# Attention with a leaky-ReLU feed-forward on one core: the feed-forward of all batches and the scores and AV of batches 3 to 8 as pairs of 64-row matmuls, and PSUM as four double banks

## The chip, the cores and the metric

The kernel runs on one core of a Trainium2 chip. A core has a matrix engine (PE), which reads weights (PEld) and streams a second operand past them into PSUM, and four others: VectorE (DVE), ScalarE (ACT), GpSimd (POOL, here mostly an issuer of DMAs and of memsets) and SyncE (SP, here an issuer of DMAs). Each has its own queue of instructions and works it off in order. PSUM has eight banks of 128 partitions x 512 fp32.

The metric is the device time of one execution in microseconds; a lower number is better. The time quoted for a kernel is the median of its runs.

## The reference

Eight batches of eight heads of attention with a relative-position bias, then a feed-forward on 4608 tokens:

```python
scores = scale * np.matmul(q, k.transpose(0, 1, 3, 2))          # q, k, v: (8, 8, 576, 64)
bias = bias_table[bucket]                                       # bucket of |i - j|; one value from distance 128 on
scores = scores + bias.transpose(2, 0, 1)[None]
attn = softmax(scores)                                          # exp(s - max) / (sum + 1e-9)
x = np.matmul(attn, v).transpose(0, 2, 1, 3).reshape(4608, 512)
h = x @ w_in                                                    # w_in: (512, 2048)
out = np.maximum(0.01 * h, h) @ w_out                           # w_out: (2048, 512)
```

All inputs and the output are fp32 in HBM; the kernel works in bf16 with fp32 sums.

## The kernel before

The attention runs over 32 items n: batch n // 4 and a pair of heads, n % 4. The two heads of a pair lie in the lower and the upper 64 partitions of `qt` and `kt` (head dimension on the partitions, 576 positions on the free axis). For an item:

- `rows`, `turn_by_pe` or `turn_by_dma`, `take_turned`: q and k are turned so that the head dimension lies on the partitions, by the PE up to item 8 (but 7) and by DMA transposes on SP's queue from then on.
- `score(n, u)`, six units: u = 0 to 3 are 128 keys each against queries 0 to 511, two matmuls of 64 rows x 512 columns, one for each head, into two banks of one `ps_s` buffer (L424). u = 4 is queries 512 to 575 of both heads, four matmuls of 128 rows x 128 columns, where `own` has zeroed the other head's half (L428). u = 5 is the last 64 keys of both heads, one matmul of 128 rows x 512 columns and one of 64 columns (L431, L432).
- `expo` (ACT): exp out of PSUM into `at` and `at4`; `band` (DVE): times exp(bias) in the band of 128 around the diagonal.
- `av`: for both heads e five chunks of queries, each four matmuls of 128 rows (keys) x 65 columns (64 of v, one of ones for the sum; L493). The last 64 keys come from `av_tail` as ten matmuls of 64 rows (L478) in items 4 to 30, and in the other items as 128-row matmuls that have zeros in the other head's half of `v4` (L496). One head's sums go to `ps_o`, the other's to `ps_o` or `ps_om`.
- `norm` (DVE): a reciprocal and a product for each head, into `opair`. Then `x_pe` and `x_copy` (items 0 to 5, 7 and 31) or `x_dma` (a DMA transpose on SP's queue) put it into `xT`, 512 features in four chunks of 128 partitions, all 4608 tokens.

The feed-forward runs over nine tiles T of 512 tokens. `ffn_in(T, f)`: four matmuls of 128 rows x 512 columns for each of 16 chunks f (L536), `ffn_act` on ACT into `gt`. `ffn_out(T, ts, i)`: for each of four groups of 128 tokens, 16 matmuls of 128 rows x 512 columns (L561), four to a step i; `ffn_y` on DVE copies the sum to SBUF, `ffn_store` writes it to HBM by SP's queue. The last group of tokens is cut into columns (`ffn_end`, L547).

PSUM has two `ps_s` buffers of two banks each, one bank `ps_o` and three single banks (`ps_m_pool`, tag "m") that hold `ps_om`, the turned tiles and all sums of the feed-forward.

The order on PE, ACT, DVE, POOL and SP is written out ahead of the run by `Plan`: each piece of work is a task (`add`) with an engine, a cost, the tasks it comes after, a rank, and the PSUM slots that it takes and gives ("S", "O", "M"). `Plan.order` places tasks by their time of readiness and rank; `SHIFT`, `HOLD` and `SWAP` correct single tasks by their number. The hardware then runs the written order with semaphores. While attention goes on, steps of the feed-forward stand on the PE between units of attention; what is left of it follows the last item. Up to 26 us, matmuls on `junk` (`spin`, L814) fill waits of the PE.

## Time and profile before

| | |
|---|---|
| median of 3 runs | 375.99 us (375.4 to 376.88) |
| the profiled execution's own time | 375.4 us |
| its span | 373.5 us |
| ACT busy | 243.7 us (65%) |
| DVE busy | 204.0 us (55%) |
| output stores (SP's queue), each 256 KB | 35, median 2.0 us to landing |
| turns of q and k by DMA | 24, median 6.2 us to landing |
| `xT` by DMA | 24, median 3.1 us to landing, 10.9 us at most |

A row of groups in the profile has the line, the engine, the operation, what it writes and reads with the shape, how often (x), its busy time, the mean duration of one in ns, and the idle time of its engine ahead of it. A matmul's duration is longer than the distance to the next one, since matmuls overlap in the array; rows of the timeline show starts, from which distances can be taken. In a row of the timeline that stands for several matmuls (x8), the time is from the start of the first to the end of the last.

### The profile page before, as it was taken

The page shows a single profiled execution, that of the slowest core. Times are in us where ns is not written, and L with a number is a line of the kernel's source. Part 1 is how long each engine was busy: PE and PEld are TensorE (multiplying, and loading weights), DVE is VectorE, ACT ScalarE, POOL GpSimd, SP SyncE. Part 2 cuts the span into 40 slices and gives each one's busy share as a digit, 9 for nine tenths or more (in the row PEclk, how much of TensorE's full clock was granted, in tenths as well). Part 3 has the DMA queues.
Part 4 walks back from the last instruction along what each step waited for, and adds up shares of the span by engine and source line. Part 5 has one row for each costly group of instructions (what it writes and reads, how often), then busy time and mean ns, then how long its engine had stood idle before and what let it go on. Part 6 is the DMA issues. An engine that isn't in the chain of part 4 may idle for free.

```text
span 373.5 us, 8628 instructions
## 1 busy us (share of the span) xinstructions
PE 368.0 (99%) x3556; PEld 191.7 (51%) x3556; DVE 204.0 (55%) x550; ACT 243.7 (65%) x351; POOL 69.4 (19%) x107
## 2 busy tenths in 40 slices
PE   8999999999999999999999999999999999999996
PEld 5675555545555555545555555545555544444444
DVE  7997567786786557655755676555643311001021
ACT  5998987588756995697667866977678333333300
POOL 8856023340025003500350013000000000000000
PEclk9999999999999999999999999999999999999999
DMA  8999999999469907991899159201210101001012
GB/s 121 156 181 197 185 181 114 212 212 176 64 132 183 177 18 111 189 157 20 131 198 146 30 113 137 71 11 47 75 47 20 47 28 54 32 28 58 28 56 86
DMA packets 103735, 39.51 MB, mean 106 GB/s; under 512 B 83472, under 2 KB 98192, under 8 KB 103696
## 3 DMA queue, kind: packets, MB, share of 16 engines
q0 software_dynamic: 53424, 18.21, 46.2%
q1 hardware_dynamic: 49920, 20.39, 29.1%
q8 instruction: 28, 0.46, 0.5%
q10 hardware_dynamic: 352, 0.36, 0.3%
q14 instruction: 11, 0.09, 0.1%
HBM read 36.70 MB, written 9.44 MB: 124 GB/s over the span
## 4 chain that ended last, share of the span: by engine, by line
PE 95%; ACT 3%; DVE 1%; issue 1%; POOL 0%; POOLq 0%
PE pm L536 34%; PE pm L561 33%; PE ps_s L424 9%; PE ps_om L493 6%; PE ps_o L493 5%; ACT at L438 2%; PE ps_s L428 2%; PE ps_s L431 2%; PE pm L547 1%; PE ps_o L478 1%; PE ps_tx L520 1%; PE ps_t L382 0%; DVE hots L301 0%; PE ps_t L387 0%; PE ps_w L814 0%
## 5 line engine op out<-in xcount | busy, mean ns | idle before, releaser
L438 ACT ACTIVATE at<-ps_s 128x1024 bf16<-128x1024 f32 x124 | 120.4, 1028 | 32.8 <-PE ps_s L424 32.8
L536 PE MATMUL pm<-xT,w_in_sb 128*128 128x512 bf16 x576 | 140.8, 379 | 0.0
L561 PE MATMUL pm<-w_out_sb,gt 128*128 128x512 bf16 x560 | 135.5, 379 | 0.0
L540 ACT ACTIVATE gt<-pm 128x512 bf16<-128x512 f32 x144 | 84.8, 605 | 59.8 <-PE pm L536 58.8
L458 DVE TENSOR_TENSOR at<-at,hk 128x768 bf16<-128x768 bf16 (+4 forms) x156 | 69.5, 453 | 64.0 <-ACT at L438 47.1
L561 PEld LDWEIGHTS <-gt 128*128 128x128 bf16 x560 | 52.5, 98 | 64.7 <-issue 5.1
L536 PEld LDWEIGHTS <-w_in_sb 128*128 128x128 bf16 x576 | 52.2, 98 | 63.1 <-issue 6.4
L566 DVE COPY y<-pm 128x512 f32<-128x512 f32 x35 | 24.2, 691 | 70.6 <-PE pm L561 70.6
L236 POOL DMA_DIRECT2D vn<-in_v_dram x32 | 28.9, 911 | 141.3 <-PE ps_o L493 131.0
L493 PEld LDWEIGHTS <-at 128*128 128x128 bf16 x1240 | 41.2, 98 | 3.7 <-issue 0.7
L424 PE MATMUL ps_s<-qt,kt 64*128 64x512 bf16 x256 | 40.0, 381 | 0.3
L440 ACT ACTIVATE at<-ps_s 128x512 bf16<-128x512 f32 x31 | 18.7, 602 | 16.7 <-PE ps_s L428 16.6
L493 PE MATMUL ps_o<-vn,at 128*128 128x65 bf16 x640 | 25.5, 193 | 0.0
L493 PE MATMUL ps_om<-vn,at 128*128 128x65 bf16 x600 | 24.1, 195 | 0.0
L424 PEld LDWEIGHTS <-kt 64*128 64x128 bf16 x256 | 8.3, 94 | 24.7 <-issue 22.0
L445 ACT ACTIVATE at<-ps_s 128x576 bf16<-128x576 f32 x31 | 20.3, 654 | 0.8 <-PE ps_s L432 0.7
L506 DVE TENSOR_TENSOR opair<-ps_o,rcp 128x320 bf16<-128x320 f32 (+2 forms) x34 | 16.4, 482 | 1.2
L506 DVE TENSOR_TENSOR opair<-ps_om,rcp 128x320 bf16<-128x320 f32 (+2 forms) x32 | 15.4, 481 | 1.1
L399 DVE COPY kt<-tu 128x576 bf16<-128x576 bf16 x24 | 15.9, 663 | 0.0
L399 DVE COPY qt<-tu 128x576 bf16<-128x576 bf16 x23 | 15.0, 652 | 0.0
L505 DVE RECIPROCAL rcp<-ps_om 128x5 f32<-128x5 f32 (+2 forms) x32 | 6.1, 192 | 15.3 <-PE ps_om L493 15.3
L228 POOL DMA_DIRECT2D kn<-in_k_dram x17 | 12.1, 715 | 9.0 <-DMA w_in_sb<-in_moe_w_in_dram 3.9
(86 smaller groups left out, 238.3 us busy)
## 6 DMA issues: line engine op xcount, KB each, us to landing
out_dram<-y SPq DMA_DIRECT2D x35, 256.0 KB, 2.0
vn<-in_v_dram POOLq DMA_DIRECT2D x32, 128.0 KB, 6.9
qn<-in_q_dram POOLq DMA_DIRECT2D x14, 288.0 KB, 10.4
kn<-in_k_dram POOLq DMA_DIRECT2D x14, 288.0 KB, 10.8
w_in_sb<-in_moe_w_in_dram POOLq DMA_DIRECT2D x2, 1024.0 KB, 11.5
w_out_sb<-in_moe_w_out_dram POOLq DMA_DIRECT2D x2, 1024.0 KB, 19.6
qn<-in_q_dram POOLq DMA_DIRECT2D x4, 144.0 KB, 4.0
v<-in_v_dram POOLq DMA_DIRECT2D x16, 32.0 KB, 7.4
```

What stands on the lines that cost most here:

```text
L236: nc.gpsimd.dma_start(out=vn[i][:, c, :, 0:D], in_=v[b, :, c * P : (c + 1) * P, :].rearrange("h s d -> s h d"),)
L399: copy(out=t[:, 0:S].rearrange("p (r c) -> p r c", c=NC), in_=src)
L424: nc.tensor.matmul(ps[:, e, :], lhsT=kt[r, u * P : (u + 1) * P], rhs=qt[r, 0:512], start=True, stop=True)
L438: nc.scalar.activation(at[:, :, u, 0:512], ps, AF.Exp, scale=scale)
L445: nc.scalar.activation(at4[:, 0:S], ps.rearrange("p e i -> p (e i)")[:, 0:S], AF.Exp, scale=scale)
L458: nc.vector.tensor_tensor(out=o, in0=o, in1=m, op=ALU.mult)
L493: nc.tensor.matmul(ps[:, ic, :], lhsT=at[:, o : o + P], rhs=vn[i][:, c, 2 * p + e, :], start=whole and c == 0, stop=not whole and ic == NJ ...
L506: nc.vector.tensor_tensor(out=opairs[n][:, lo:hi, e * D : (e + 1) * D], in0=ps[:, lo:hi, 0:D], in1=rcp.to_broadcast([P, hi - lo, D]), op=A ...
L536: nc.tensor.matmul(pms[T, f], lhsT=w_in_sb[:, c, f * P : (f + 1) * P], rhs=xT[c][:, t0 : t0 + w], start=(c == 0), stop=(c == n_cc - 1))
L540: nc.scalar.activation(gts[T][:, f, :], pms.pop((T, f)), AF.Prelu, bias=0.0, scale=1.0, alpha=0.01)
L561: nc.tensor.matmul(ys[T, ts], lhsT=gts[T][:, f, ts * P : (ts + 1) * P], rhs=w_out_sb[:, f, :], start=(f == 0), stop=(f == n_fc - 1))
L566: nc.vector.tensor_copy(out=y, in_=ys[T, ts])
```

## The change

1. **Feed-forward.** x is held as eight chunks `xT[:, j, :]`: the lower 64 partitions have head j, the upper 64 the other head of its pair, so each head stands in both halves. It is a ring of four batches and no longer holds all eight. `w_in_sb` has the weights of the first eight f in its lower half and those of the last eight in its upper half, with the heads in the same order. `ffn_in(T, f)` makes 8 pairs of 64-row matmuls: the lower gives chunk f, the upper chunk f + 8, in two banks; `ffn_act` takes both at once (1024 columns, eight times a tile). `ffn_out` makes two partial sums, one for each half of the rows, in two banks; `ffn_half` (ACT) copies one to SBUF and `ffn_y` (DVE) adds the other.
2. **Scores.** u = 4 is eight 64-row matmuls of 64 columns in all items. u = 5 from item 8 on is two turns of two 64-row matmuls of 288 columns; in the second turn each half writes the bank that the other wrote in the first. `own` is no longer applied to q.
3. **AV.** From item 8 to 30, `av_half`: two turns of 40 64-row matmuls; in turn 0 each half of the rows serves one head, in turn 1 the other. `av_tail` starts every item with ten 64-row matmuls. Both heads go to one double bank. Items 0 to 7 and 31 keep 128-row matmuls (`av_full`).
4. **Guard between turns.** Both halves write the same bank in turn, so that turn 1 must not begin before turn 0 has ended. `look` (DVE) reads one element of a later score unit out of PSUM (unit 2 of the next item for AV, unit 3 for u = 5), and turn 1 waits for it.
5. **x.** `norm` takes both heads at once. By DMA (now items 4 to 31) `swap_heads` (DVE) makes a copy with the heads swapped, and two transposes are issued. By PE (items 0 to 3) there is a second turn of ten transposes of 64 columns each and a second copy. From batch 4 on the transposes come after the `ffn_in` that reads the part of the ring that they overwrite.
6. **PSUM.** Four tiles of two banks each; slots are given out by number, "S" and "O" of two banks, "M" and "N" of one in the first part. AV takes an "S" slot from item 16 on.
7. `load_w_in` issues three DMAs for each half and not one; `y` has three buffers and not four; `SHIFT`, `HOLD` and `SWAP` are new for the new numbers of tasks.

```diff
+    RING = 4
+    xT = per.tile([P, H, RING * S + P - SL], BF16, name="xT")
+    w_in_sb = per.tile([P, H, DF // 2], BF16, name="w_in_sb")
+    pairs_ = [ps_pool.tile([P, 2, 512], FP32, name=f"ps{i}") for i in range(4)]
...
+        if u == NJ:
             for c in range(NJ):
-                nc.tensor.matmul(ps[:, 0, c * P : (c + 1) * P], lhsT=kt[:, c * P : (c + 1) * P],
-                                 rhs=qt[:, S : S + P], start=True, stop=True)
+                for e in range(2):
+                    r = slice(e * D, (e + 1) * D)
+                    nc.tensor.matmul(ps[:, e, c * SL : (c + 1) * SL], lhsT=kt[r, c * P : (c + 1) * P],
+                                     rhs=qt[r, 512:S], start=True, stop=True)
...
+    def score_tail(n, turn):
...
+        for e in range(2):
+            r, x = slice(e * D, (e + 1) * D), (e + turn) % 2
+            nc.tensor.matmul(ps[:, x, 0:HS], lhsT=kt[r, S : S + P], rhs=qt[r, x * HS : (x + 1) * HS],
+                             start=(turn == 0), stop=(turn == 1))
+
+    def look(n, u):
+        nc.vector.tensor_copy(out=mark, in_=scores[n, u][0:1, 0, 0:1])
...
+    def av_half(n, turn, ics):
...
+        ps = outs[n] if turn else av_tail(n, ics)
+        for ic in (ics if turn == 0 else reversed(ics)):
             for c in range(NJ):
+                for g in range(2):
+                    e = (g + turn) % 2
+                    r = slice(g * SL, (g + 1) * SL)
+                    o = (e * NJ + c) * S + ic * P
+                    nc.tensor.matmul(ps[:, e, ic * W1 : (ic + 1) * W1], lhsT=at[r, o : o + P],
+                                     rhs=vn[i][r, c, 2 * p + e, :], start=False,
+                                     stop=turn == 1 and ic == ics[0] and c == NJ - 1)
...
+    def swap_heads(n):
+        o = opairs[n]
+        t = swapped[n] = op_pool.tile([P, NJ + 1, 2 * D], BF16, name="swapped")
...
-            out=xT[p][:, b * S : b * S + w].rearrange("p (i t) -> p i t", t=P),
-            in_=opairs[n].rearrange("p i d -> p (i d)"),
+            out=xT[:, 2 * p + e, b % RING * S : b % RING * S + w].rearrange("p (i t) -> p i t", t=P),
+            in_=(opairs, swapped)[e][n].rearrange("p i d -> p (i d)"),
...
+        for j in js:
+            for g in range(2):
+                r = slice(g * D, (g + 1) * D)
+                nc.tensor.matmul(pms[T, f][:, g, :], lhsT=w_in_sb[r, j, f * P : (f + 1) * P], rhs=x_cols(T, r, j),
+                                 start=(j == 0), stop=(j == H - 1))
...
+        nc.scalar.activation(gts[T][:, f::HF, :], pms.pop((T, f)), AF.Prelu, bias=0.0, scale=1.0, alpha=0.01)
...
         for f in range(4 * i, 4 * i + 4):
-            nc.tensor.matmul(ys[T, ts], lhsT=gts[T][:, f, ts * P : (ts + 1) * P], rhs=w_out_sb[:, f, :],
-                             start=(f == 0), stop=(f == n_fc - 1))
+            for g in range(2):
+                r = slice(g * D, (g + 1) * D)
+                nc.tensor.matmul(ys[T, ts][:, g, :], lhsT=gts[T][r, f, ts * P : (ts + 1) * P], rhs=w_out_sb[r, f, :],
+                                 start=(f == 0), stop=(f == n_fc - 1))
+
+    def ffn_half(T, ts):
+        outs["y"] = y_pool.tile([P, DM], FP32, name="y")
+        nc.scalar.copy(out=outs["y"], in_=ys[T, ts][:, 1, :])
 
     def ffn_y(T, ts):
-        y = y_pool.tile([P, DM], FP32, name="y")
-        nc.vector.tensor_copy(out=y, in_=ys[T, ts])
+        y = outs.pop("y")
+        nc.vector.tensor_tensor(out=y, in0=ys[T, ts][:, 0, :], in1=y, op=ALU.add)
...
+            if u == 2 and split:
+                mk = add("DVE", 0.1, [t], lambda: look(n, 2), rank - 30)
+                split[1]["after"].append(mk)
+                split[1]["proof"] = mk
+            if u == 3 and not tail5:
+                mk = add("DVE", 0.1, [t], lambda: look(n, 3), rank - 30)
+                t5 = add("PE", 0.13, [t, mk], lambda: score_tail(n, 1), first, proof=mk)
...
+            sw = add("DVE", 0.3, [nm], lambda: swap_heads(n), soon + 4)
+            xt[n] = [add("SP", 0.1, [d], lambda e=e: x_dma(n, e), soon + 4, tail=6.0) for e, d in ((0, nm), (1, sw))]
...
+            half = add("ACT", 0.53, last_p + ([yts[-3]] if len(yts) > 2 else []), lambda ts=ts: ffn_half(T, ts), 0)
+            y = add("DVE", 0.65, last_p + [half], lambda ts=ts: ffn_y(T, ts), 0, give=["O"], of=[(o, 0)])
```

More of the change, by code (lines that the diff above doesn't have):

```diff
@@ L74, in link @@
             t["after"] = [d for d in t["after"] if not any(d is o for o in t["behind"])]
+            if t["give"] and not t["of"]:
+                t["of"] = [(next(d for d in t["after"] if d["take"]), j) for j in range(len(t["give"]))]
     def order(self):
@@ L122, in order @@
             held = {k: sorted(slots[k]) for k in set(t["take"])}
-            r = max([r] + [s[t["take"].count(k) - 1] for k, s in held.items()])
+            r = max([r] + [s[t["take"].count(k) - 1][0] for k, s in held.items()])
             ring = self.place(t, r, free, slots, ring)
@@ L136, in place @@
         t["idle"] = r - free.get(e, 0.0)
+        t["room"] = min([x for k in "SMNO" for x in slots[k]], key=lambda x: x[0], default=(1e9, 0))
+        if t["room"][0] > free.get(e, 0.0) + 0.1:
+            t["room"] = None
         free[e] = r + cost
+        t["got"] = []
         for k in t["take"]:
[L139 to L141 removed]
+            x = min(slots[k])
+            slots[k].remove(x)
+            t["got"].append(x[1])
+        for k, (o, j) in zip(t["give"], t["of"]):
+            slots[k].append((t["end"] + self.LAG, o["got"][j]))
         return ring
@@ L148, in run @@
                 k = round(t["idle"] / 0.22) if t["start"] < 8.5 else int((t["idle"] - 0.1) / 0.11)
-                if k > 0:
-                    fill(k)
+                if k > 0 and t["room"]:
+                    fill(k, t["room"][1])
+            self.now, made = t, len(self.code())
             t["go"]()
+            if t["engine"] in ("ACT", "DVE"):
+                t["code"] = self.code()[-1]
+            elif t["proof"]:
+                self.follow(self.code()[made], t["proof"]["code"])
 @with_exitstack
@@ L704, in plan_pair @@
+            if u < 5 or tail5:
+                es[u] = add("ACT", ac[u], [t], lambda u=u: expo(n, u), rank + 2, give=spent if u == 4 else ["S"], of=[(t, 0)])
+        if not tail5:
+            ss.append(t5)
         sct[n] = ss
@@ new lines, in plan_turns @@
+        def plan_turns(after, at, ics):
+            lo, hi = ics[0] * P, min(ics[-1] * P + P, S)
+            w, xs, cs = len(ics) / 5, [], []
+            for turn in range(2):
+                x = add("PE", (0.36, 0.4)[turn] * w, after, lambda turn=turn: x_pe(n, turn, ics), at + 1, take=["M"], wide=True)
+                t = add("DVE", 0.07 + 0.35 * w, [x], None, at, give=["M"], of=[(x, 0)])
+                t["go"] = lambda t=t, turn=turn: x_copy(n, turn, t, lo, hi)
+                t["other"] = ("ACT", 0.22 + 0.31 * w)
+                xs.append(x)
+                cs.append(t)
+            return xs, cs
```

372 lines of the change are left out of this document (200 added, 172 removed), and 18 rows, old and new, of tables (HOLD, SHIFT).

## The prediction

> **What bounds the kernel now.** I read the page's shares and its chain of waits first, then the windows, then the timeline of the PE over one item.
>
> ```profile
> PE 368.0 (99%) x3556; PEld 191.7 (51%) x3556; DVE 204.0 (55%) x550; ACT 243.7 (65%) x351; POOL 69.4 (19%) x107
> ...
> PE 95%; ACT 3%; DVE 1%; issue 1%; POOL 0%; POOLq 0%
> ```
>
> The PE holds 95% of the chain that ended last. Its busy share proves little, since a matmul's duration covers the start of the next, so I look at distances between starts in one item of the steady stage.
>
> ```profile
> 117.84 0.77 PE L493 MATMUL ps_o<-vn,at 128*128 128x65 bf16 x20
> 118.45 1.89 PE L536 MATMUL pm<-xT,w_in_sb 128*128 128x512 bf16 x8
> 120.18 0.39 PE L428 MATMUL ps_s<-qt,kt 128*128 128x128 bf16 x4
> 120.40 0.38 PE L431 MATMUL ps_s<-qt,kt 128*128 128x512 bf16 x1
> 120.61 0.19 PE L432 MATMUL ps_s<-qt,kt 128*128 128x64 bf16 x1
> 120.64 1.89 PE L536 MATMUL pm<-xT,w_in_sb 128*128 128x512 bf16 x8
> 122.47 0.60 PE L424 MATMUL ps_s<-qt,kt 64*128 64x512 bf16 x4
> 123.00 2.76 PE L536 MATMUL pm<-xT,w_in_sb 128*128 128x512 bf16 x12
> 125.70 0.60 PE L424 MATMUL ps_s<-qt,kt 64*128 64x512 bf16 x4
> 126.14 0.19 PE L478 MATMUL ps_o<-v,at 64*128 64x65 bf16 x1
> 126.15 0.19 PE L478 MATMUL ps_om<-v,at 64*128 64x65 bf16 x1
> ...
> 126.26 0.19 PE L478 MATMUL ps_o<-v,at 64*128 64x65 bf16 x1
> 126.27 0.19 PE L478 MATMUL ps_om<-v,at 64*128 64x65 bf16 x1
> 126.39 0.79 PE L493 MATMUL ps_om<-vn,at 128*128 128x65 bf16 x20
> 127.01 0.77 PE L493 MATMUL ps_o<-vn,at 128*128 128x65 bf16 x20
> 127.62 1.24 PE L536 MATMUL pm<-xT,w_in_sb 128*128 128x512 bf16 x5
> ```
>
> An item repeats after 9.17 us (118.45 to 127.62). Its prices:
> - 128 x 512: the eight from 118.45 are over at 120.18, so 0.216 us each. 28 of them: 6.05.
> - Units 4 and 5 of the scores: 120.18 to 120.64, 0.46; unit 4 alone (four of 128 columns) 0.22.
> - A change between 128 and 64 rows: 120.64 + 8 x 0.216 = 122.37, but the 64-row scores start at 122.47; two pairs of them at 0.216 would end at 122.90, but the feed-forward starts at 123.00. So 0.10 each way, and again at 125.59 to 125.70 and 126.29 to 126.39: four in an item, 0.40.
> - A pair of 64-row matmuls costs what one 128-row matmul does: its halves start 0.01 or less apart (126.14, 126.15). Pairs of 65 columns: 126.14 to 126.26 is four, 0.030 each. Pairs of 512: 125.70 to 126.14 is two, 0.22 each by rows that round to 0.01.
> - AV: 40 of 128 rows, 126.39 to 127.62, 1.23, or 0.031 each; tail five pairs, 0.15.
>
> Sum: 6.05 + 0.46 + 0.40 + 4 x 0.216 + 1.23 + 0.15 = 9.15 of 9.17. The item is PE work and nothing else.
>
> ```profile
> core 0: us, PE busy (x) PEld busy (x) DVE busy (x) ACT busy (x) POOL busy (x), PEclk, DMA share, GB/s
> 118.45:127.62 9.17, 9.17 (x99) 4.65 (x96) 5.18 (x16) 8.21 (x14) 0.00 (x0) 1.00 1.36 205
> 31.93:370.50 338.57, 338.57 (x3035) 170.99 (x3031) 176.80 (x460) 217.16 (x313) 46.06 (x60) 1.00 0.70 101
> 31.93:118.45 86.52, 86.52 (x895) 44.91 (x892) 62.50 (x168) 64.91 (x91) 25.67 (x34) 1.00 1.30 164
> ```
>
> The same prices laid on the whole written order from the first feed-forward matmul (31.93) to the last matmul give 338 us, and the stage took 338.57. The granted clock (PEclk) is 1.00 throughout. So under 1 us of the stage is waiting, and anything taken off the PE's order there comes off the time, as long as no wait replaces it.
>
> **The change part by part.** The sum goes against the profiled execution's 375.4 us.
>
> *Items 8 to 30, 23 of them.* Everything is in 64 rows, so all four changes of rows go: -0.40. Unit 4 becomes four pairs of 64 columns, by the 65-column pairs 0.030 each: 0.22 to 0.12, -0.10. Unit 5 was 0.24 and becomes two pairs of 288 columns; by columns 288/512 x 0.216 = 0.12 each, 0.24: nothing. Tail and AV: 1.38 becomes 45 pairs at 0.030, 1.35: -0.03. Together -0.53, or **-12.2 us**. Unknown is a run of 98 small matmuls where the trace shows ten: its bounds are 0.015 for one matmul (half of the 0.030 above) and the distance of narrow 128-row matmuls,
>
> ```profile
> 7.56 1.01 PE L318 MATMUL ps_u<-diag,hots 128*128 128x32 bf16 x32
> L318 PE MATMUL ps_u<-diag,hots 128*128 128x32 bf16 x96 | 3.3, 177 | 0.2 <-DVE hots L301 0.2
> ```
>
> (1.01 - 0.18) / 31 = 0.027. I take 0.015, the nearest row in shape and rows.
>
> *Feed-forward.*
>
> ```profile
> L536 PE MATMUL pm<-xT,w_in_sb 128*128 128x512 bf16 x576 | 140.8, 379 | 0.0
> L561 PE MATMUL pm<-w_out_sb,gt 128*128 128x512 bf16 x560 | 135.5, 379 | 0.0
> ```
>
> These 1136 matmuls become 1136 pairs. A pair of 512 columns lies between 0.216 and the 0.22 to 0.23 that the roundings allow (two pairs and a change in 0.53, 122.47 to 123.00). I take 0.216, since the 128-row price also is pure column count (128 columns 0.055, 512 columns 0.216): 0 us, with an upper bound of 1136 x 0.01 = +11. Speaking against it, the Trainium skill ("TensorE: Matmul & The Clock Gate", section "The mechanism") says that weight loads overlap running matmuls only where the row group differs; consecutive pairs use the same two groups. By that rule each pair would show its load, at most the 0.030 of a small pair, and the sum would be 34 higher; but in the tail two loads and two matmuls on the same groups fit into 0.030 with nothing added, so the trace does not agree with it.
>
> *Items 4 to 7 and 31.* Unit 4: 5 x -0.10. They keep two to four changes of rows, about as before, save that 31 loses about two (-0.2). The PE transposes of x for 4, 5, 7 and 31 go to DMA: 20 transposes at 0.055, -1.1. Together **-1.8**.
>
> *Items 0 to 3.* Ten more narrow transposes each, about 0.28 by five of 128 columns: +1.1; some 14 more changes of rows: +1.4; unit 4: -0.4; so +2.1 on the PE. Here the PE is not full:
>
> ```profile
> 29.67 0.20 PE L496 MATMUL ps_o<-v,at 128*128 128x65 bf16 x1 [0.72 <-issue]
> 30.06 0.18 DVE L505 RECIPROCAL rcp<-ps_o 128x4 f32<-128x4 f32 x1 [1.00 <-PE ps_o L496]
> L524 DVE COPY xT<-ps_tx 128x576 bf16<-128x576 bf16 x6 | 2.7, 450 | 1.5 <-PE ps_tx L520 1.5
> L814 PE MATMUL ps_w<-junk 128*128 128x256 bf16 x36 | 6.8, 324 | 1.2 <-DVE junk L261 1.2
> ```
>
> There is the 0.72 wait and filler work on junk, that can shrink. But the second turn and the second copy (0.45) stand in the chain ahead of the first feed-forward. From 0 to +2.5; I take **+1.2**.
>
> *Guards.* Turn 1 of AV and of unit 5 wait on PE for a DVE read, 47 times. Path: a 512-column matmul lasts 0.38, so its end is 0.16 past the next start; 0.04 to the DVE (29.83 + 0.19 to 30.06 for a waiting reciprocal); the smallest read of PSUM 0.18 (that row); back about 0.06: 0.44. In the built order 41 of the 47 have eight or more feed-forward matmuls in between (four pairs, 0.86) and cost nothing while the DVE is free; without that cover each would cost 0.44. Six have at most one narrow pair (0.12): 0.32, and for a DVE busy 5.18 of 9.17 with operations near 0.5 another 0.14: 6 x 0.46 = 2.8. For covered ones that meet a late DVE, 0.7. **+3.5**, bounds 1.9 (six at 0.32) and 47 x 0.46 = 22. Queued behind a waiting turn 1 is the whole PE order; late next is the slot that this score or AV holds.
>
> *ACT and DVE.*
>
> ```profile
> L438 ACT ACTIVATE at<-ps_s 128x1024 bf16<-128x1024 f32 x124 | 120.4, 1028 | 32.8 <-PE ps_s L424 32.8
> L540 ACT ACTIVATE gt<-pm 128x512 bf16<-128x512 f32 x144 | 84.8, 605 | 59.8 <-PE pm L536 58.8
> L566 DVE COPY y<-pm 128x512 f32<-128x512 f32 x35 | 24.2, 691 | 70.6 <-PE pm L561 70.6
> L403 DVE TENSOR_TENSOR qt<-qt,own 128x128 bf16<-128x128 bf16 x32 | 7.0, 219 | 0.1
> ```
>
> ACT: 72 of 1.03 for 144 of 0.605, -11; 35 half copies at about 0.6, +21: 254 us in all, +10. Hidden under the PE as a total, though in this item ACT is busy 8.21 of 9.17; a shorter item leaves it some 0.4 of slack. DVE: `own` on q -7, 47 reads +8, 28 swaps at about 0.5 +14: 220 in all. Off the path, price in the rivals. The `ffn_y` sum waits for the ACT copy, which holds a double bank about 0.6 longer; the other "O" slot covers with 1.73 of matmuls.
>
> *DMA.* SP's queue issues 56 transposes of x in place of 24, each ahead of turns, stores and further transposes.
>
> ```profile
> xT<-opair SPq DMA_TRANSPOSE x24, 3.1
> DMA to landing us min/median/max: 2.5/3.1/10.9
> L512 SPq DMA_TRANSPOSE xT<-opair x24: 1199/1206/3375, 63.6 to 289.7; - x24
> ```
>
> Each holds the queue 1.2 us. Where it matters is tile 1, which needs items 4 to 7; until 118 us the DMA share is 1.30. The feed-forward of tile 0 (27.6 us) and the next items cover it: in the built order some 10 us of PE work stand between AV of item 7 and tile 1. Nothing, with 0 to +5. The extra issues of w_in on POOL are hidden by the same work.
>
> Sum: 375.4 - 12.2 - 1.8 + 1.2 + 3.5 = 366.1. The profiled run is 0.6 under the median shown (375.99), so I forecast **366.5 us**.
>
> **The rivals.**
> - *Guards and slots eat it.* Half of the covered guards meet a busy DVE, or ACT with its 0.4 of slack gives the four double banks back late: 47 x 0.2 = +9, 375.5, no change. For it: every item has two guards and the DVE order is strict. Against: 0.42 to spare on 41 of 47. Chance 0.12.
> - *Feed-forward pairs are not 0.216* but 0.22 to 0.226: +4.5 to +11, 371 to 377. For it: the 0.22 by rows. Against: two pairs to their end leave no room for more than 0.004 each. 0.09; and 0.01 for weight loads shown in full, 0.030 at each pair, +34, 400 (the skill's rule above).
> - *Slower: small 64-row matmuls have a floor per matmul, not per pair.* In a long run the queue empties and 98 small matmuls an item go at 0.027, as L318 does, not 0.015: 23 x 98 x 0.012 = +27, 393. It decides from 0.019 on (9 us / 2254 = 0.004 above 0.015). For it: L318 and L493 never go under 0.027 a matmul, and the ten at 0.015 follow 0.44 of scores, in which a queue can fill. Against: those ten hold the rate to the end. The Trainium skill ("TensorE: Matmul & The Clock Gate", section "Wait — 56ns, not 53.3ns?") states a floor of about 25 ns from start to start however narrow; the tail's 0.01 or less inside a pair does not agree. 0.07.
> - *x comes late* in the loaded stage: one stall of 3 to 6, 371. 0.07.
>
> **How the numbers follow.** Forecast 0.64, with its own range 362.5 to 370 (guards at 1.9 and start at 0 give 363; guards and start dearer 370). The range 362 to 376 takes in late x, most of the dearer pairs and half of the eaten gain, and leaves out the floor and the upper ends. What a measurement of this kernel tells from no change is about 0.5%, 1.9 us. Faster: 0.64 + 0.07 + 0.07 + 0.02 = 0.80; within: 0.07; slower: 0.13, the floor and the upper ends of guards and pairs.
>
> **What would show it.** An item of 32 feed-forward pairs lasting 9.5 us (6.91 + 2.57); 64-row groups of eight feed-forward matmuls (four pairs) starting 0.86 apart; 80 AV matmuls of an item in 1.20 without their pause; no 0.10 ahead of scores from item 8 on; first feed-forward matmul near 33 us; waits of the PE for the DVE read in six places only. Wrong it would be with PE idle ahead of AV's second turn in most items, AV turns of 40 at over 0.75 us, or PE waiting for ACT at the scores.

## The result, and the profile after

| | before | after |
|---|---|---|
| median (lowest to highest) | 375.8 us (375.4 to 376.88) | 402.38 us (400.61 to 403.68) |
| the profiled execution | 375.4 us, span 373.5 | 401.42 us, span 399.6 |

The ratio is 1.0699, with a 95% interval of 1.0646 to 1.0753: the change made the kernel 26 us slower, where 9 us faster was forecast. (Here and below ratios leave disturbed runs out, so they can differ a little from the ratio of two medians.)

The page of after, in order: 40 slices of 10 us for PE, granted clock and DMA engines, the queue of SP's DMAs, the chain that ended last.

```profile
PE   8999999761799999799999999999999999999997
...
PEclk9999999995799999899999999999999999999999
DMA  8999999999386999999399969922223401010112
...
q1 hardware_dynamic: 71424, 25.64, 40.7%
...
PE 78%; ACT 9%; DMA 8%; DVE 3%; issue 1%; SPq 0%; ACTq 0%
```

The page of before has this row for that queue:

```profile
q1 hardware_dynamic: 49920, 20.39, 29.1%
```

The PE's share of the chain fell from 95% to 78%; a DMA came into it, and ACT's share grew. The hole lies in the slices of 70 to 110 us, the clock lowered in the last two. The queue has 5.25 MB more in 32 more transposes. The time of its packets, added up and divided by 16 engines, is 40.7% of 399.6 us against 29.1% of 373.5, so 54 us more, or 1.7 for each added transpose. That is not time in which a transpose has the engines to itself: packets overlap (in the windows below such sums reach 1.65 of a stretch), and the stores of this queue took longer too.

The windows of after, cut where the stages change (columns as in the prediction's windows):

```profile
0.00:39.24 39.24, 35.97 (x587) 23.63 (x588) 29.07 (x86) 27.86 (x38) 26.84 (x52) 1.00 1.65 159
39.24:76.00 36.76, 35.77 (x519) 20.19 (x517) 24.02 (x62) 32.83 (x41) 12.38 (x16) 1.00 1.50 161
76.00:108.50 32.50, 15.96 (x256) 7.85 (x250) 9.60 (x23) 11.63 (x15) 2.70 (x4) 0.74 1.29 125
108.50:160.00 51.50, 50.24 (x969) 28.95 (x967) 36.83 (x100) 42.38 (x52) 7.75 (x10) 1.00 1.08 138
160.00:167.00 7.00, 4.95 (x74) 2.47 (x72) 4.10 (x10) 4.86 (x7) 6.05 (x9) 0.76 1.29 87
167.00:396.50 229.50, 226.44 (x3427) 119.19 (x3424) 106.45 (x248) 140.43 (x167) 15.34 (x19) 1.00 0.58 91
```

Between 76 and 108.5 us the PE is busy for half of the time. Now the account. The first feed-forward matmul moved from 31.93 to 39.24 us: +7.3. From there to the last matmul before took 338.5 us and after 357.2: +18.7. Both together are the 26.0 between the profiled executions. The written order of that stretch, laid out with the prediction's prices for each kind of matmul, shrank from 337.8 to 324.1, by 13.7, much as forecast. So some 32 us are new waits and lost clock: 19.8 at 76 to 108 us; about 4 at 160 to 167, which begin at a guard; 6.6 at the other guards (eight with full cover at 0.65 each, the rest 1.4); 1.7 at 42 to 60, where PE turns wait for ACT.

One item of the steady stage, in the timeline of the PE:

```profile
205.75 0.60 PE L460 MATMUL ps<-qt,kt 64*128 64x512 bf16 x4
206.19 1.89 PE L625 MATMUL ps<-xT,w_in_sb 64*128 64x512 bf16 x16
207.91 0.32 PE L531 MATMUL ps<-v,at 64*128 64x65 bf16 x10
208.06 0.79 PE L558 MATMUL ps<-vn,at 64*128 64x65 bf16 x40
208.67 0.40 PE L460 MATMUL ps<-qt,kt 64*128 64x512 bf16 x2
...
215.26 0.60 PE L460 MATMUL ps<-qt,kt 64*128 64x512 bf16 x4
```

From 205.75 to 215.26 are 9.51 us, with 64 feed-forward matmuls, 32 pairs. Eight pairs take 1.72 (206.19 to 207.91), 0.215 each; 40 AV matmuls take 0.61 (208.06 to 208.67), 0.030 a pair; a pause ahead of the 64-row scores is gone.

The hole, in the timelines of after; the bracket at the end of a row is the wait ahead of it and what ended it. PE:

```profile
79.07 0.39 PE L460 MATMUL ps<-qt,kt 64*128 64x512 bf16 x2 [2.06 <-DVE kt L435]
...
87.84 0.23 PE L466 MATMUL ps<-qt,kt 64*128 64x64 bf16 x4 [2.27 <-issue]
...
91.35 0.61 PE L625 MATMUL ps<-xT,w_in_sb 64*128 64x512 bf16 x2 [2.65 <-DMA xT<-opair]
95.77 0.61 PE L625 MATMUL ps<-xT,w_in_sb 64*128 64x512 bf16 x2 [3.81 <-DMA xT<-swapped]
102.12 1.89 PE L625 MATMUL ps<-xT,w_in_sb 64*128 64x512 bf16 x8 [5.74 <-DVE y L663]
```

DVE, and the queue of SP:

```profile
100.83 0.65 DVE L435 COPY qt<-tu 128x576 bf16<-128x576 bf16 x1 [16.18 <-DMA tu<-pr]
```

```profile
61.92 2.76 SPq L409 DMA_TRANSPOSE tu<-pr  x1
64.73 5.48 SPq L585 DMA_TRANSPOSE xT<-opair  x1
70.32 6.16 SPq L585 DMA_TRANSPOSE xT<-swapped  x2
...
85.68 5.91 SPq L409 DMA_TRANSPOSE tu<-pr  x1
```

Two waits name the transposes of x; for one (2.27) the profile names nothing. The last names a sum on DVE, which stood behind a copy that waited 16.18 us for a turned q (`tu`): that turn was issued behind two transposes of x, and each issue here held SP for 2.7 to 5.9 us, where the prediction had 1.2. Long issues aren't new. The queue of SP in before has them in this stage too:

```profile
64.85 5.12 SPq L373 DMA_TRANSPOSE tu<-pr  x1
```

New is what stands ahead of the turns: by 76 us after had issued six transposes of x and two turns, before one and five. So the hole opens after five of the additional transposes, not 32. The five waits are 16.5 of the 19.8; the rest is short waits and the clock, which was granted at 0.50 from 92 to 104 us.

### The profile page after: what moved, and what is told of

It is laid out like the page before. It is cut to its first block, busy times and chain, and to the rows that moved or that the text cites. A ratio compares the mean times of both kernels' runs of the same rounds, so it can differ in the third digit from the quotient of the medians.

```text
span 399.6 us, 13183 instructions
## 1 busy us (share of the span) xinstructions
PE 369.6 (92%) x5808; PEld 202.3 (51%) x5808; DVE 210.1 (53%) x528; ACT 260.2 (65%) x316; POOL 71.1 (18%) x107
## 3 DMA queue, kind: packets, MB, share of 16 engines
q1 hardware_dynamic: 71424, 25.64, 40.7%
## 4 chain that ended last, share of the span: by engine, by line
PE 78%; ACT 9%; DMA 8%; DVE 3%; issue 1%; SPq 0%; ACTq 0%
PE ps L625 28%; PE ps L654 27%; DMA tu<-pr 8%; PE ps L558 7%; PE ps L460 7%; ACT at L493 5%; PE ps L941 2%; PE ps L483 2%; ACT gt L631 2%; PE ps L543 1%; PE ps L531 1%; PE ps L638 1%; DVE hk L343 1%; ACT qt L435 1%; PE ps L466 1%
## 5 line engine op out<-in xcount | busy, mean ns | idle before, releaser
L625 PE MATMUL ps<-xT,w_in_sb 64*128 64x512 bf16 x1152 | 144.0, 382 | 12.2 <-DVE y L663 5.7
L493 ACT ACTIVATE at<-ps 128x1024 bf16<-128x1024 f32 x124 | 124.8, 1029 | 32.6 <-PE ps L460 25.0
L654 PE MATMUL ps<-w_out_sb,gt 64*128 64x512 bf16 x1120 | 134.8, 376 | 0.0
L631 ACT ACTIVATE gt<-ps 128x1024 bf16<-128x1024 f32 x72 | 74.2, 1031 | 44.2 <-PE ps L625 44.2
L625 PEld LDWEIGHTS <-w_in_sb 64*128 64x128 bf16 x1152 | 57.1, 95 | 72.3 <-issue 18.0
L516 DVE TENSOR_TENSOR at<-at,hk 128x768 bf16<-128x768 bf16 (+4 forms) x156 | 68.0, 452 | 40.7 <-ACT at L493 28.5
L654 PEld LDWEIGHTS <-gt 64*128 64x128 bf16 x1120 | 54.7, 94 | 56.0 <-issue 0.3
L460 PE MATMUL ps<-qt,kt 64*128 64x512 bf16 x256 | 48.4, 397 | 3.0 <-DVE kt L435 2.3
L558 PE MATMUL ps<-vn,at 64*128 64x65 bf16 x1840 | 35.9, 190 | 1.9 <-DVE mark L487 1.5
L558 PEld LDWEIGHTS <-at 64*128 64x128 bf16 x1840 | 32.5, 94 | 7.9 <-DVE mark L487 4.7
L570 DVE TENSOR_TENSOR opair<-ps,rcp 128x640 bf16<-128x640 f32 (+2 forms) x34 | 26.7, 785 | 1.2
```

The source lines that it names most:

```text
L460: nc.tensor.matmul(ps[:, e, :], lhsT=kt[r, u * P : (u + 1) * P], rhs=qt[r, 0:512], start=True, stop=True)
L493: nc.scalar.activation(at[:, :, u, 0:512], ps, AF.Exp, scale=scale)
L516: nc.vector.tensor_tensor(out=o, in0=o, in1=m, op=ALU.mult)
L558: nc.tensor.matmul(ps[:, e, ic * W1 : (ic + 1) * W1], lhsT=at[r, o : o + P], rhs=vn[i][r, c, 2 * p + e, :], start=False, stop=turn == 1 an ...
L570: nc.vector.tensor_tensor(out=opairs[n][:, lo:hi, e0 * D : e1 * D].rearrange("p i (e d) -> p e i d", d=D), in0=ps[:, :, :, 0:D], in1=rcp.t ...
L625: nc.tensor.matmul(pms[T, f][:, g, :], lhsT=w_in_sb[r, j, f * P : (f + 1) * P], rhs=x_cols(T, r, j), start=(j == 0), stop=(j == H - 1))
```

## The experiments

All 16 kernels that ran stand here. Each is compared with the kernel before on the same chip (375.6 to 376.4 us).

### Which part makes the hole

Theory: the second transposes of x. First they are left out, the feed-forward reading the first chunk twice. Then the kernel before gets as many additional transposes that nobody reads. Then the second copy is made by DVE across partitions.

```diff
 def x_cols(T, r, j):
+    j = j - j % 2 if T > 0 else j
 def x_dma(n, e):
+    if e == 1: return
```

> The changed kernel without the second transpose of x (28 DMAs left out, the copy on DVE stays); from tile 1 on the feed-forward reads the plain chunk twice, so this part of the result is left out. PE, ACT and DVE have the same order. Theory (the doubled transposes hold SP's queue from 62 to 92 us, 2.7 to 5.9 us each, and the turns of q and k behind them come late): the PE's wait between 76 and 105 us (18 us in the changed kernel) goes to under 5, the wait at 160 to 167 goes too, time 378 to 384. Rival (the loads by POOL's queue fill the DMA engines there, whatever SP issues): the wait stays over 10, time over 392.

Measured: 382.37 us (382.23 to 387.53), ratio 1.022 [1.011, 1.032]. By the medians 20 us come off. The execution with a profile is the slowest (387.53), 13.9 below that of after, and all of this comes out of the hole: waits of 1.2 and 2.0 ahead of 84.18 and 87.25 us are left, with the halved clock some 6 us of 19.8. The stall that after has at 160 to 167 us did not go, against the theory. After, then this run:

```profile
162.44 0.30 PE L483 MATMUL ps<-qt,kt 64*128 64x288 bf16 x2 [1.36 <-DVE mark L487]
```

```profile
147.72 0.30 PE L483 MATMUL ps<-qt,kt 64*128 64x288 bf16 x2 [1.36 <-DVE mark L487]
```

In both, the guard's read waits 1.40 us for ACT's exponential, and 0.69 for ACT follow. So the second transposes don't make this stall.

```diff
# the kernel before
-    y_pool = ctx.enter_context(tc.tile_pool(name="y", bufs=4))
+    y_pool = ctx.enter_context(tc.tile_pool(name="y", bufs=3))
 def x_dma(n):
+    x_again(n, 1)        # the same transpose into a scratch tile
 def x_copy(n, ...):      # for the turns by PE of items 4 to 31
+    x_again(n, 2)
```

> The kernel before with as many transposes of x on SP's queue as the changed kernel has (56 from item 4 on; the added ones write scratch that nobody reads), and three y buffers. Theory (transposes alone make the turns late): PE waits of 8 to 20 us between 60 and 110, time 384 to 396. Rival (the wait is the changed kernel's own, from its order or its shorter items): time under 379.

Measured: 388.38 us (388.14 to 389.59), ratio 1.034 [1.030, 1.038]: +12.6. In the timeline of its PE:

```profile
77.19 1.02 PE L547 MATMUL pm<-xT,w_in_sb 128*128 128x512 bf16 x4 [1.88 <-DVE xT L533]
...
95.42 1.03 PE L425 MATMUL ps_s<-qt,kt 64*128 64x512 bf16 x4 [7.86 <-DVE kt L400]
```

The kernel before, with these transposes and three y buffers like the changed kernel, shows a hole at the same place; behind the wait of 7.86 stands DVE's copy of a turned q, which waited 8.65 us for its DMA. So neither pairs nor guards nor double banks are needed for it. (The y buffers weren't changed alone; no long wait there names them.) The packet time of SP's queue is 37.2% of 386.4 us here, 35 us above before: 1.1 for each of the same 32 transposes, where after had 1.7.

```diff
+c1 = add("DVE", 0.3, [], lambda: x_across(n, 0), soon + 4)
 d = add("SP", 0.1, [nm], lambda: x_dma(n, 0), soon + 4, tail=6.0)
+c2 = add("DVE", 0.3, [d], lambda: x_across(n, 1), soon + 4)
```

> The changed kernel with the second copy of x made by two DVE copies across the halves of the partitions, from what the first transpose has put down, in place of the swapped copy and the second transpose; the written order shifts with it. Theory (the second transpose is what costs): waits between 76 and 105 us under 6, time 378 to 386, like the kernel that leaves the second transpose out. Rival (DVE, now waiting for a DMA in its queue, hands the delay on to the guards and bands): time over 392.

Measured: 413.02 us (411.15 to 414.5), ratio 1.098 [1.092, 1.105]. The rival held: DVE, in order, now waits for a transpose's landing (six waits, 23.6 us in all), with all that is queued behind it.

### Queue or DMA engines

SP's queue could be what is short, or the DMA engines behind it. First the second transposes go to ACT's queue.

```diff
-nc.sync.dma_start_transpose(
+(nc.sync, nc.scalar)[e].dma_start_transpose(
```

> Base is the kernel after (402.4 us). Each second transpose of x is issued by ScalarE in place of SyncE, at the same place of the planned order; nothing else. Theory: what delays the turned q and k is SyncE's queue, in which 56 transposes of x stand in place of 24; with two queues the wait at 76 to 105 us shrinks to a few us and the time is 385 to 392. Rival: the transposes are slow on the shared DMA engines, whoever issues them: 398 or more, and ScalarE's exponentials stand behind the issues, which would make it slower than 402.

Measured: 523.75 us (522.34 to 524.58), ratio 1.393 [1.390, 1.397]. In the built program every transpose on one queue waits until those on the other have landed, so the edit brought a wait of its own (up to 12 us on ACT) and doesn't decide. The Trainium skill ("DMA: Bandwidth & Descriptors", section "Latency and other measured facts") says that two transposes in flight on different queues corrupt each other and must be serialized; the waits in the program agree, and no run here shows the corruption.

Then the loads of batch 3, which share the DMA engines with the transposes, are held back until item 9's last score. The gated loads are those of q and k at 57.7 to 64.2 us (the expectation misnames them); v of batch 3 and q and k of batch 4 moved along, and all ran at 84 to 98 us.

```diff
 def load_qk(b, h0, h1, js=(0, 1)):
+    if b == 3 and not gate:
+        late.append((b, h0, h1)); return
 def score_tail(n, turn):
+    if n == 9 and turn == 1:
+        gate.append(plan.code()[-1])
+        for a in late: load_qk(*a)
```

> Base is the kernel after (402.4 us). The four loads of batch 3's q and k (288 KB each, issued at 76 to 85 us there, first read at 109 us) wait for the tail of item 9's scores; same instructions in the same order otherwise. Theory: between 60 and 105 us the DMA engines are full, and the turns and x transposes land late because these loads share the engines with them; without them the turn of item 10 lands some 8 us sooner, TensorE's waits of 18 us in 76 to 108 us shrink to 10 or less, and the time falls to 388 to 395. Rival: the order on SyncE's queue alone is what is late; 400 to 403.

Measured: 401.22 us (399.95 to 404.91), ratio 1.069 [1.064, 1.075]. Its windows, then its PE and its SP:

```profile
60.00:80.00 20.00, 19.71 (x318) 11.25 (x314) 13.81 (x34) 16.65 (x21) 0.00 (x0) 1.00 0.73 131
...
110.00:120.00 10.00, 6.69 (x50) 2.50 (x49) 2.75 (x7) 2.44 (x5) 5.74 (x8) 0.83 1.91 129
120.00:130.00 10.00, 0.00 (x0) 0.00 (x0) 0.00 (x0) 0.00 (x0) 0.67 (x1) 0.68 1.42 169
```

```profile
132.08 1.04 PE L467 MATMUL ps<-qt,kt 64*128 64x512 bf16 x4 [12.70 <-DVE kt L442]
```

```profile
62.70 1.30 SPq L416 DMA_TRANSPOSE tu<-pr  x1
...
103.56 10.80 SPq L416 DMA_TRANSPOSE tu<-pr  x2
```

With the loads gone from 60 to 84 us, the same 56 transposes in the same order hold SP for 1.2 to 1.3 us there, and the hole at 76 to 108 is closed. It opens again behind the loads, once as 12.70. So the count on SP's queue isn't what makes the hole: transposes and loads of q, k and v do, where they meet.

### The late start

Rivals: a clock that comes late, the second turn and copy of x, and double banks that are one tile. In after's start, DVE's copy of kt (second bank of a pair) waits for ACT's copy of qt (first bank), and two matmuls of scores still last 0.61 us at 17 to 19 us, against 0.39 in before from 8.5 us on. The granted-clock column can't tell here: the trace of after has no clock record ahead of 19.94 us (before: 4.57), and the column shows 1.00 where there is none. ACT, DVE and PE of after:

```profile
6.71 0.64 ACT L435 COPY qt<-ps 128x576 bf16<-128x576 bf16 x1 [1.16 <-PE ps L418]
```

```profile
7.38 0.76 DVE L435 COPY kt<-ps 128x576 bf16<-128x576 bf16 x1 [1.11 <-ACT qt L435]
```

```profile
16.80 0.61 PE L460 MATMUL ps<-qt,kt 64*128 64x512 bf16 x2
```

and the PE of before:

```profile
8.52 0.39 PE L424 MATMUL ps_s<-qt,kt 64*128 64x512 bf16 x2
```

```diff
-spin(10, 0)
+spin(24, 0)
```

> The changed kernel with 24 matmuls on junk at the start and not 10, which delays the first work by some 3 us. Theory (in the changed kernel the granted clock is full only from 20.0 us, before from 4.6 us, and the half clock makes the first feed-forward come at 39.2 and not 31.9): full clock by 9 us, first feed-forward at 35 to 37, time 397 to 400. Rival (the start is late by the second turn of x and by fewer PSUM banks): full clock early, but the first feed-forward at 39 or later, time 401 or more.

Measured: 385.8, 394.46 and 397.04 us, too far apart for a ratio, but all below the lowest run of after (400.61). The first feed-forward matmul came at 42.1 us, 2.8 later than in after, so the start didn't gain. The hole did: two waits are left, 0.93 and

```profile
94.49 1.89 PE L625 MATMUL ps<-xT,w_in_sb 64*128 64x512 bf16 x8 [6.61 <-DVE y L663]
```

The DMAs are the same in the same order. So a start some 3 us later is enough to change the hole by several us. Edits that move the start or the loads do this too, and of differences of a few us between the runs below none is put down to one cause by its time alone.

```diff
# on the first experiment: items 0 to 3 too (x_copy likewise)
 def x_pe(n, turn, ...):
+    if turn == 1: return
```

> Base e1 (382.4 us, first feed-forward matmul at 38.99 us), now with the second part of x of items 0 to 3 left out too (TensorE turn and copy); the feed-forward reads the first part in both row groups, so that part of the result is left out. Theory: the late start is not the second part of x itself but the two halves of a double bank waiting for each other, and the clock that is lost there; only some 1.6 us of TensorE work goes, so the first feed-forward matmul comes near 37 us and the time near 380. Rival: the second part is what delays the start: first feed-forward matmul by 34 us, time 377 or less.

Measured: 389.79 us (386.87 to 393.77), ratio 1.034 [1.029, 1.039]. The first feed-forward matmul came at 37.10, 1.9 before the first experiment's 38.99, but the waits at 81 to 89 us grew, to 1.29 and 5.41.

```diff
-pairs_ = [ps_pool.tile([P, 2, 512], FP32, name=f"ps{i}") for i in range(4)]
+pairs_ = [ps_pool.tile([P, 2, 512], FP32, name=f"ps{i}") for i in range(2)] + [None, None]
+singles[g, h] = one_pool.tile([P, 512], FP32, ...)   # g = 2, 3; two-bank tiles from the hand-over on
```

> Base is the kernel after (402.4 us, first feed-forward matmul at 39.24 us). The two double banks of the start (turned q and k, the table, turned x) are four tiles of one bank each until they are handed to the feed-forward; same instructions in the same order, but a half no longer waits for the other half's copy. Theory: the waits between the halves cost most of the late start: first feed-forward matmul by 35 us, first exponential near 7.5 us, time 4 us less or more (398 or below). Rival: TensorE is only late because its clock is half until 20 us, or because of the second turn of x: first feed-forward matmul stays at 38 us or later and the time at 400 to 403.

Measured: 401.15 us (398.81 to 403.41), ratio 1.067 [1.062, 1.072]. Its DVE and its PE:

```profile
6.70 0.76 DVE L446 COPY kt<-one 128x576 bf16<-128x576 bf16 x1 [0.44 <-PE one L429]
```

```profile
84.50 0.39 PE L636 MATMUL ps<-xT,w_in_sb 64*128 64x512 bf16 x2 [3.68 <-DMA xT<-swapped]
90.47 0.61 PE L636 MATMUL ps<-xT,w_in_sb 64*128 64x512 bf16 x2 [4.91 <-DMA xT<-opair]
94.30 0.61 PE L636 MATMUL ps<-xT,w_in_sb 64*128 64x512 bf16 x2 [3.22 <-DMA xT<-swapped]
100.98 1.89 PE L636 MATMUL ps<-xT,w_in_sb 64*128 64x512 bf16 x8 [6.07 <-DVE y L674]
```

With the same order and one tile to a bank, DVE waits for the PE alone and the first feed-forward matmul starts at 36.19, 3.05 earlier. The gain is given back whole: the same transposes are waited for, 17.9 us in place of 16.5, and the group at 102.12 starts at 100.98.

A part of the 3.05 is the clock. Of the nine other traces with two-bank tiles at the start, eight have clock records of 0.50 for 7 to 14 us between 11 and 26 us (the first experiment: 12.8 to 19.6). Of the six with one-bank tiles none has it there. The ninth with two-bank tiles (late loads without guards, below) has 1.00 from 10.5 us on and starts its feed-forward at 37.64, between the 38.6 to 40.0 of those with the same start and the halved clock and the 35.2 to 36.2 of the one-bank runs (but 38.39 in the one with the reads put ahead, below, whose clock is halved from 31.8 to 35.2). So, as an estimate from these starts, some 1 to 2 us are the waits between halves, and about as much is the clock.

### The guards

On the first experiment, the second turns are let run without the read, each adding to the banks of its first turn.

```diff
-mk = add("DVE", 0.1, [t], lambda: look(n, 3), rank - 30)
-t5 = add("PE", 0.13, [t, mk], lambda: score_tail(n, 1), first, proof=mk)
+t5 = add("PE", 0.13, [t], lambda: score_tail(n, 1), first)
```

> Base e1 (382.4 us). The 47 guards are left out: the second turns of the score tail and of AV add to the same bank as the first turns, so no bank gets two row groups; the same matmuls in the same order, the cross terms of tail and AV go to the wrong head. Theory: the guards still cost some 8 us in all (eight to eleven waits of 0.65 us and the six short ones), so 374 to 376, and no wait of 0.4 us or more is left after 110 us on TensorE. Rival: the waits only stand where TensorE would have waited for ACT a moment later anyway: 380 to 382.

Measured: 382.48 us (382.35 to 383.18), ratio 1.017 [1.015, 1.019], against 382.37 with guards. The executions with a profile differ more, 383.18 against 387.53: from 113 us to the end some 6 us are gained, ahead of it 2 lost (at 82 to 94 us 7.7 are lost, with guards 5). The faster executions with guards (382.2 and 382.4) have no trace, so what the guards cost in them stays open. Of the stall at 147 us, waits of 1.05 and 0.25 for ACT are left. Why covered guards cost anything shows in after, in the rows of PE, ACT and DVE around 173 us:

```profile
172.11 0.28 PE L483 MATMUL ps<-qt,kt 64*128 64x288 bf16 x2
172.23 0.38 PE L460 MATMUL ps<-qt,kt 64*128 64x512 bf16 x2
172.45 1.02 PE L654 MATMUL ps<-w_out_sb,gt 64*128 64x512 bf16 x8
173.96 0.30 PE L483 MATMUL ps<-qt,kt 64*128 64x288 bf16 x2 [0.49 <-DVE mark L487]
```

```profile
172.70 1.02 ACT L493 ACTIVATE at<-ps 128x1024 bf16<-128x1024 f32 x1 [0.23 <-PE ps L460]
```

```profile
173.76 0.14 DVE L487 COPY mark<-ps 1x1 f32<-1x1 f32 x1 [0.94 <-ACT at L493]
```

The read waits 0.94 us for ACT's exponential of the same unit, which stands ahead of it in the program and reads the same banks; that is longer than the 0.86 of cover. 16 of the 47 reads are ordered so. The Trainium skill ("PSUM — Partial Sum Buffer", section "PSUM bank collisions raise a hardware error") says that two engines may not touch one bank at once, reads included, and that software orders them; the wait in this trace (0.94) agrees.

The test of that mechanism puts each read ahead of the exponential, in the kernel with one-bank tiles and paced loads that comes below:

```diff
 def expo(n, u):
+    if (n, u) in want: look(n, u)
```

> e13 (two undisturbed runs at 386.7 and 392.0 us) with one thing changed: a guard's DVE read stands ahead of the exponential that reads the same bank, no longer behind it. In the kernel after, 16 of the 47 reads wait in the program for ACT's exponential of the same unit (1.03 us), since DVE and ACT take turns on a bank; 1.03 + 0.44 less the cover of 0.86 is the 0.6 that the late guards show. Theory: no guard waits above 0.3 us are left on TensorE after 110 us (e14 shows what their absence is worth: 386.2 to 391.7), so 386 to 391. Rival: the guards are late because the DVE stands behind earlier work; the waits of 0.65 us stay, some now on ACT, 389 to 394.

Measured: 390.44 us (387.72 to 390.91), ratio 1.036 [1.031, 1.040], against 1.035 without the edit. Of the waits at covered guards one is left (0.60, ahead of 154.81 us), and 0.75 of the wait at 162.44. Now ACT waits for the read, which this row of its table of waits shows (sum in us, count, longest):

```profile
ACT at L531 <- DVE mark L522: 27.3, 27, 3.6
```

So the order of the read and the exponential does make those waits, and the time didn't move when it was turned round.

### Taking causes away together

The held-back loads were combined with one-bank tiles, with no second transposes, and with neither second transposes nor guards, by the edits shown above.

> e9 and e8 together: late loads of batch 3, and the banks of the start as tiles of one bank. Theory: the 3 us that e8 won at the start were lost again because the next stage ended at the pace of the DMA engines; if the late loads relieve that stage, part of the 3 us stays: 2 to 3 us below e9. Rival: the transposes themselves set the pace of that stage, and e10 is within 1 us of e9.

> e1 (no second transpose of x; 382.4 us) with the late loads of e9. Theory: e1's waits of 3.4 us at 82 to 87 us and the half clock after them (1.4 us) go: 377 to 380. Rival: 381 to 383.

> e6 (no second transpose of x, no guards; 382.5 us) with the late loads of e9: against e11 it gives the price of the 47 guards where the loaded stage no longer hides it. Theory: 5 to 7 us below e11 (the stretch from 113 us to the end was 6.3 us shorter in e6's profile than in e1's): 371 to 374. Rival: the guards are covered, within 1 us of e11.

Measured: 396.63 us (395.5 to 398.14), ratio 1.056 [1.052, 1.059]; 394.06 (390.65 to 395.33), 1.047 [1.042, 1.053]; 387.66 (386.49 to 394.33), 1.030 [1.027, 1.034]. Where the transposes no longer bind at 76 us, one-bank tiles keep 4.6 us, the first feed-forward matmul coming 4.1 earlier. Leaving the guards out is worth 6.4 by the medians; between the profiled executions it is 3.4, of which 1.6 is an earlier start that has no guards in it. The last two missed their forecasts by 14 us: without second transposes late loads are worse than the first experiment by 12, and the longest wait, 4.81 us ahead of 121.36, is for the turned k of a later item.

So the loads of batches 3 to 5 were spread, each behind an item, on one-bank tiles; then without guards; then without second transposes too.

```diff
+GATE = {("qk",3,0): 8, ("qk",3,1): 9, ("v",3): 10, ("qk",4,0): 11, ("qk",4,1): 12, ("v",4): 14, ("qk",5,0): 15, ("qk",5,1): 16}
 def score_tail(n, turn):
+    if turn == 1:
+        open_[n] = plan.code()[-1]
+        for key, go in held.pop(n, []): paced(key, go)
```

> e8 (one-bank tiles at the start, 401.2 us) with the loads of batches 3 to 5 spread out: each group of q and k and each of v waits for the score tail of a fixed item (8, 9, 10, 11, 12, 14, 15, 16); same instructions in the same order. In e9 and e10 the gated loads were those of batch 3, issued at 58 to 64 us in the kernel after, and the groups behind them moved along, so all came at once at 84 to 98 us and the wait of 13 us came at 113 to 132 us. Theory: transposes are late only where loads crowd the DMA engines; spread out, no wait of TensorE above 4 us is left, the waits of 18 us shrink to 6 or less, and the time is 380 to 388. Rival: the transposes and loads together are more than the DMA engines can move in 40 to 150 us, however they are spread: the waits stay near 15 us, 393 or more.

> e13 without the 47 guards (second turns add to the banks of the first turns: cross terms of tail and AV go to the wrong head). Theory: with no other wait to hide them the guards cost 5 to 8 us, so this is 5 to 8 us below e13. Rival: within 1 us of e13, the guards are covered or their time comes back as another wait.

> All four losses out together: no second transpose of x (e1), one-bank tiles at the start (e8), no guards (e6), loads paced (e13); the feed-forward reads the first part of x in both row groups and the cross terms of tail and AV go to the wrong head. Theory: what is left is the written order of TensorE, some 13.7 us shorter from the first feed-forward matmul on than before, and a start that is 2 to 5 us later: 364 to 371, faster than before. Rival: the order itself is no shorter on the chip than the sum of its rows says, or another wait takes the place of these: 376 or more.

Measured: 393.06 us (386.65 to 395.02), ratio 1.035 [1.026, 1.044]; 389.43 (386.19 to 391.71), 1.035 [1.029, 1.041]; 381.96 (378.73 to 383.35), 1.017 [1.014, 1.020]. Pacing is worth some 8 us against one-bank tiles alone by the medians and 12 by the ratios. Without guards the median is 3.6 lower and the ratio the same, so nothing clear of the spread came of it. With every named cause out the kernel is still not faster: its time is the rival's. Waits in the PE's timeline of that last one:

```profile
116.12 1.04 PE L659 MATMUL ps<-xT,w_in_sb 64*128 64x512 bf16 x8 [2.29 <-DVE opair L601]
...
166.21 0.29 PE L562 MATMUL ps<-v,at 64*128 64x65 bf16 x4 [3.29 <-DVE at L546]
```

Its profiled execution, the fastest of the four at 378.73, adds up: 375.4, -13.7 for the order, +3.8 for a first feed-forward matmul at 35.68 instead of 31.93, and 13 of waits like these. So the shorter order is there, and what is fed to it on time isn't. No version ran that beats the kernel before.

## Why the prediction was wrong, step by step

- *Items 8 to 30, -12.2, and items 4 to 7 and 31, -1.8*: right. An item with 32 feed-forward pairs takes 9.51 us where 9.5 was foretold, and the whole order is 13.7 shorter. The price of 0.216 holds, so the rival of dearer pairs falls, and with 0.030 for an AV pair in runs of 40 the slower rival, a floor per matmul, falls too.
- *DMA, "Nothing, with 0 to +5"*: the step that failed most. It priced each issue at the median of 1.2 us, though its own row goes up to 3.375 and before's turns to 5.12 in this stage; it took "the feed-forward of tile 0 (27.6 us) and the next items" for enough cover; and it left out that the DMA engines are already busy there (its own window has a share of 1.30 up to 118 us) and that the turns of q and k queue behind x. Measured: 19.8 us at 76 to 108, of which some 14 go when the second transposes are left out (20 in the time by the medians), and 12.6 on by adding transposes to the kernel before. The rival "x comes late" had the place and the mechanism, but counted one stall of 3 to 6; there are five, since turns queue behind x, and DVE and PE behind the turns.
- *Items 0 to 3, "From 0 to +2.5; I take +1.2"*: failed; +7.3. The working counted the second turn and copy, and leaving those out gives 1.9 back. It left out that the two banks of a tile are ordered as one, and the clock that is halved with it: 3.05 by one-bank tiles, the clock's part included. No run has both edits; the two would leave some 2 us, and what makes that rest stays open.
- *Guards, +3.5*: right in kind, and mis-sized at 6.6, to which a part of the 4 us at 160 to 167 comes. "41 of the 47 have eight or more feed-forward matmuls in between and cost nothing while the DVE is free" left out that the read waits for an exponential; eight covered ones cost 0.65 each. Of three pairs of kernels with and without guards, one has a gain clear of the spread (6.4 by the medians), so what they cost in the time isn't settled by these runs.
- *ACT and DVE hidden*: right in the main; PE waits for ACT 1.7 us at 42 to 60 and, with the guard, at 160 to 167.
- The sum itself rested on "as long as no wait replaces it". Waits replaced it, and they also lowered the granted clock (0.74 in the window of 76 to 108.5), which no step of the prediction had considered.

Open is what is short where loads and transposes meet, the DMA engines' time or their order between the loads' packets and the transposes, since the run that was to tell it brought its own wait; how much of each gain is only a shift of that meeting; and whether another order of loads would let the 13.7 through.

## What to carry to other kernels

Price a DMA that an edit adds at the time of the DMA engines in its own stretch, not at its issue alone, and look at what is queued behind it on the issuing queue: here doubled small transposes cost more than the whole gain on the PE, and the hole opened after the first five. A shorter order on the bounding engine is worth something only while its inputs still come; compare the DMA row of that stage before counting it. Two banks held as one tile and a read used as a proof both add orderings between engines that the diff doesn't show.

## What the runs showed of the hardware that was not expected

- A transpose of 164 KB (5.25 MB / 32) added 1.1 us (kernel before with more transposes) to 1.7 us (after) of packet time over 16 engines. Its issue held SP's queue for 1.2 us with no loads running (62 to 84 us of the run with late loads) and for 2.7 to 5.9 where loads ran (61 to 96 us of after).
- 64-row AV pairs in runs of 40 matmuls kept 0.030 us a pair, 0.015 a matmul.
- Among waits of 2 to 6 us the granted clock fell to 0.50: in after from 92 to 104 us, where PE is busy for 2.5 of 12 us.
- At the start of after the PE ran at half speed by its durations (0.61 against 0.39) for 20 us. The column of granted clock shows 1.00 there only because the trace has no clock record before 19.94 us.
